# First keys in two transfers, four extra products ahead of the first transposes, and a later place for five value loads

## The chip, the cores and the metric

The kernel runs on one core of one Trainium2 chip. The metric is the device time of one execution in microseconds. TensorE (PE) multiplies, VectorE (DVE), ScalarE (ACT) and GpSimd (POOL) do the elementwise work, and transfers are issued by GpSimd's and SyncE's (SP) queues. The program is built under a manual schedule: each engine runs its instructions in the order in which the Python code issues them, and semaphores order the engines among each other.

## What is computed

Attention in a sliding window of 32 positions to either side, for 8 sequences of 576 positions with 8 heads of 64, then two matrix products with a gelu-like gate between them:

```python
def _attn_ref(q, k, v):
    scores = scale * np.matmul(q, k.transpose(0, 1, 3, 2))
    mask = np.abs(pos[:, None] - pos[None, :]) <= window      # window = 32
    scores = np.where(mask, scores, -1000000000.0)
    ...
    attn = attn / (np.sum(attn, axis=-1, keepdims=True) + 1e-09)
    return np.matmul(attn, v)

def _moe_ref(x, w_in, w_out):          # 4608 x 512, 512 x 2048, 2048 x 512
    h = x @ w_in
    g = h * (1.0 / (1.0 + np.exp(-1.702 * h)))
    return g @ w_out
```

## The kernel before

The 4608 rows (8 sequences of 576, one after the other) are cut into 36 units of 128 rows; four units make a tile of 512, nine tiles in all. For a unit, `scores` multiplies transposed keys by transposed queries, ScalarE exponentiates, `band` multiplies by a 0/1 mask, `values` multiplies by the values (with a column of ones that gives the sums), `norm` divides, `x_T` transposes the result. For a tile, layer 1 (512 to 2048) and layer 2 (2048 to 512) follow. From the second tile on both use a seven-product scheme for 2x2 blocks, whose sums VectorE forms; the first tile is multiplied plainly (`layer1_plain`, `layer2_plain`).

Queries and values are offset by 32 rows against each other. A unit's scores need keys of the unit and the first half of the next one. The values of a unit need `ve[u % 9]`, a ring of nine tiles, and `vo[u % 5]`, a ring of five that `odd_v` fills on GpSimd with the upper half of one value tile and the lower half of the next.

`opening` handles the first two tiles. `load_first` (L147) loads the keys and queries of the first tile in two parts each, several rows of a head on one partition; `setup_mask` (L99) makes the identity from an iota of GpSimd and a comparison of VectorE; `T_first` (L166) transposes on TensorE, four heads to a PSUM bank, and VectorE and ScalarE copy out. `seed` (L268) starts a score bank with a large negative bias by a product of the identity and the bias tile. `load_four` and `T_four` (L185, L193) do the same for the second tile. GpSimd issues all loads in one order: first keys, first queries, second part of both, values 0 to 4, then w_in in pieces, the second tile's keys and queries, the rest of w_in, more values, and w_out in four pieces.

Later units are loaded by `fetch(u)` (L722): queries of u, keys and values of u + 1. `T_pe` (L237) transposes units 8 to 12 on TensorE; `turn(u)` (L727) issues transposes by transfer on SyncE's queue for all later ones. `first_layer1` (L871) is layer 1 of the second tile; in its four rounds it copies odd values 8 to 11 and fetches 12 to 15. `run` (L809) then goes on with scores 8 to 15 and their values, and copies odd values 12 to 15 and fetches 16 there. `front` and `back` (L736, L764) repeat the pattern for the tiles from the third on. At most eight transfers of GpSimd are under way: each further one waits for the landing of the eighth before it. Each of the five buffers for queries and for keys comes free when its transpose has read it.

Of the kernel before, what the change touches and what calls it, by code (L numbers as in the profile page):

```python
# [15 lines left out]
F32 = mybir.dt.float32  # L16
BF16 = mybir.dt.bfloat16
# [9 lines left out]
class _Kernel:  # L27
# [55 lines left out]
    def setup(self):  # L83
        nc, cst = self.nc, self.cst
        self.ident = cst.tile([128, 128], BF16, name="ident")
        self.identh = cst.tile([128, 128], F16, name="identh")
        self.mask = cst.tile([128, 4, SQ], BF16, name="mask")
        self.bias = cst.tile([128, 512], BF16, name="bias")
        self.w1 = cst.tile([128, 4, self.DFF], F16, name="w1")
        self.w2 = cst.tile([128, 16, self.DM], F16, name="w2")  # L90
        self.a = {i: cst.tile([128, 2, 1024], F16, name=f"a{i}") for i in (1, 2, 3, 4)}
        self.b = {i: cst.tile([128, 8, 256], F16, name=f"b{i}") for i in (1, 2, 3, 4)}
        self.k_first = cst.tile([128, 4, 64], BF16, name="k_first")
        self.v_first = cst.tile([64, self.H, 66], BF16, name="v_first")
        self.ve = [cst.tile([128, self.H, 66], BF16, name=f"ve{i}") for i in range(9)]
        self.vo = [cst.tile([128, self.H, 66], BF16, name=f"vo{i}") for i in range(5)]
        self.spark = cst.tile([128, 1], F32, name="spark")

    def setup_mask(self):  # L99

        D = self.work.tile([128, 128], F32, name="gap", tag="s7", bufs=2)
        self.nc.gpsimd.iota(D, pattern=[[-1, 128]], base=0, channel_multiplier=1,
                            allow_small_or_imprecise_dtypes=True)
        dve = self.nc.vector
        dve.tensor_single_scalar(self.ident, D, 0.0, op=ALU.is_equal)
        dve.tensor_copy(self.identh, self.ident)
        for r in (slice(0, 64), slice(64, 128)):
            d = D[r, r].rearrange("p (b s) -> p b s", b=1).to_broadcast([64, 2, SQ])
            up = int(r.start > 0)
            for blk, op in ((2 * up, ALU.is_ge), (2 - 2 * up, ALU.is_le)):  # L110
                dve.tensor_single_scalar(self.mask[r, blk:blk + 2, :], d, 0.0, op=op)
# [35 lines left out]
    def load_first(self, c, part):  # L147
        if "first" not in self.stage:
            self.stage["first"] = self.sb("g", [128, self.H, 11, self.D], BF16, 2, "kq1")
        lo, n, j, at = self.FIRST[c][part]  # L150
        src = {"q": self.q, "k": self.k}[c]
        self.nc.gpsimd.dma_start(self.stage["first"][0:n // j, :, at:at + j],  # L152
                                 src[0, :, lo:lo + n, :].rearrange("h (p j) d -> p h j d", j=j))

    def kq_tile(self, t):

# [433 lines left out]

    SHARES = {("first", 1): (3, 0, 5, 4), ("first", 2): (3, 3, 6, 6), ("first", 3): (3, 1, 7, 7), ("last", 0): (0, 12, 6, 6),
              0: (4, 4, 6, 6), 1: (3, 3, 6, 6), 2: (0, 6, 5, 7), 3: (2, 1, 5, 4)}

    def opening(self):

        nc, dve, act, pool = self.nc, self.nc.vector, self.nc.scalar, self.nc.gpsimd
        self.setup()  # L600
        self.load_first("k", 0)
        self.load_first("q", 0)
        dve.memset(self.spark, 0.0)
        self.setup_mask()
        self.cut_mask()
        self.setup_bias()
        for t in self.ve:
            dve.memset(t[:, :, self.D:], 1.0)
        self.load_first("k", 1)
        self.load_first("q", 1)  # L610
        act.activation(self.spark, self.spark, AF.Exp)
        for u in (0, 1, 2, 3):
            self.load_v(u)
        self.load_v(4, slice(0, 1))
        self.load_w1(0, 256)
        self.load_w1(256, 256)
        self.load_w1(512)
        for u in (0, 1):
            self.odd_v(u, pool)
        self.load_w1(1024)  # L620
        for u in (2, 3):
            self.odd_v(u, pool)
        self.load_four("k")
        self.load_four("q")
        self.load_w1(1536)
        self.load_v(4, slice(1, 2))
        for u in (5, 6, 7, 8):
            self.load_v(u)
        for c in range(4):
            self.load_w2(c)  # L630
        self.T_first("k", 0, "AC", (dve, act))
        self.seed(0, "t")
        self.T_first("q", 0, ("LA", "LB"), (dve, act))
        self.seed(1, "AC")
        self.scores(0)
        self.scores(1)
        self.T_first("k", 1, ("LA", "LB"), (dve, dve))
        self.T_first("q", 1, ("B", "E"), (dve, act))
        self.seed(2, ("LA", "LB"))
        self.seed(3, "AC")  # L640
        self.scores(2)
        self.scores(3)
        self.values(0, "t")
        self.norm(0)
        self.values(1, ("B", "E"))
        self.norm(1)
        self.x_T(0, "LA", act)
        self.x_T(1, "LB", act)
        self.values(2, "t")
        self.norm(2)  # L650
        self.values(3, "AC")
        self.norm(3)
        h, n = ["LA", "LB", "A", "C", "B", "E"], [0]

        def l1(half, *fs, **kw):
            for f in fs:
                self.layer1_plain(0, f, half, h[n[0] % len(h)], **kw)
                n[0] += 1

        l1(0, 0)  # L660
        self.x_T(2, "B", act)
        self.x_T(3, "E", dve)
        l1(0, 2)
        l1(1, 0, 2)
        dve.tensor_copy(self.k_first, self.kT[0][:, :, 0:64])
        dve.tensor_copy(self.v_first, self.ve[0][0:64])
        l1(0, 4, 6)
        l1(1, 4, 6)
        for i in (3, 1, 2, 4):
            self.w1_sums((i,), 0)  # L670
        h[:], n[0] = ["LA", "LB", "C"], 0
        l1(0, 8)
        halo = self.kT[4]
        self.T_four("k", "BE", (dve, act))
        dve.tensor_copy(self.kT[4][:, :, 0:64], halo)
        l1(0, 10)
        act.activation(self.spark, self.spark, AF.Exp)  # L677
        self.T_four("q", "tA", (dve, act))
        gelus = []
        kept = [self.sb("s7", [128, 512], F32, 2) for _ in range(2)]  # L680
        room = self.sb("xs", [128, 2, 512], F32, 1, "room")
        kept += [room[:, i, :] for i in range(2)]
        l1(1, 8, later=gelus, kept=kept[0])
        l1(1, 10, later=gelus, kept=kept[1])
        for u in (4, 5, 6, 7):
            self.odd_v(u, pool)
        self.load_kq("k", 8)
        for u in (8, 9, 10, 11):
            self.fetch(u)
        h[:], n[0] = ["LB", "LA"], 0  # L690
        self.scores(4, "AC")
        self.scores(5, "t")
        l1(None, 12, later=gelus, kept=kept[2])
        self.scores(6, "BE")
        self.band(4)
        l1(None, 13, later=gelus, kept=kept[3])
        self.scores(7, "AC")
        self.values(4, "t")
        self.band(5)
        self.norm(4)  # L700
        h[:], n[0] = ["B", "E"], 0
        l1(None, 14, later=gelus)
        self.band(6)
        l1(None, 15, later=gelus)
        self.values(5, "t")
        self.norm(5)
        self.band(7)
        self.values(6, "AC")
        self.do(self.l2, 6)
        self.do(gelus)  # L710
        self.norm(6)
        self.values(7, "t")
        self.norm(7)
        self.do(self.l2, 2)
        for i in (3, 1, 2):
            self.w1_sums((i,), 1)
        self.x_T2(4, "A", act)
        self.do(self.l2, 8)
        self.x_T2(6, "t", dve)
        self.do(self.l2, 6)  # L720

    def fetch(self, u):  # L722
        self.load_kq("q", u)
        self.load_kq("k", u + 1)
        self.load_v(u + 1)

    def turn(self, u):  # L727
        self.T_dma("q", u)
# [35 lines left out]
    def back(self, t):  # L764
# [3 lines left out]
        u = 4 * t + 4  # L768
        bands = [lambda i=i: self.band(u + i) for i in range(4)] if more else []
        dv = bands[0:2]  # L770
        for n in range(4):
            self.turn(u + n + 4)
            self.fetch(u + n + 5)
            if t == 2 and n in (1, 3):
                self.values(u + n - 1, "t")
                self.norm(u + n - 1)
# [32 lines left out]
    def run(self):  # L809
        pool, act = self.nc.gpsimd, self.nc.scalar  # L810
# [20 lines left out]
        do(more, 4)  # L831
        self.values(8, "t")
        self.values(9, "AC")
        self.odd_v(12, pool)
        self.odd_v(13, pool)
        self.fetch(16)
        self.scores(11, "BE")
        self.norm(8)
        self.band(10)
# [16 lines left out]
        self.scores(15, "t")  # L856
        do(self.x_sums(2))
        self.seed2 = dve
        self.odd_v(14, pool)
        self.odd_v(15, pool)  # L860
        late = self.back(2)
        for t in range(3, self.NT):
            self.front(t, late)
# [7 lines left out]
    def first_layer1(self):  # L871

        dv = [lambda: self.w1_sums((4,), 1)]
        for n in range(4):
            if n == 3:
                self.turn(12)
                self.turn(13)
            self.odd_v(8 + n, self.nc.gpsimd)
            self.fetch(12 + n)

            def fill(i):
                self.do(self.l2, {1: 1, 7: 1, 2: 3, 4: 3}[i])
# [55 lines left out]
```

## Time and profile before

| | |
|---|---|
| three timed runs | 283.83, 285.00, 285.83 us |
| median | 285.0 us |
| profiled execution, its own time | 282.94 us |
| its span, first to last instruction | 281.2 us |
| instructions | 8890 |
| DVE busy | 212.2 us (75%) |
| ACT busy | 196.0 us (70%) |
| POOL busy | 132.1 us (47%) |
| software queue (GpSimd's), moved | 18.42 MB in 106656 packets |
| hardware queue (SyncE's and ScalarE's), moved | 18.10 MB in 43120 packets |
| output stores, 256 KB each, to landing | 4.8 us |

The page gives each engine's busy time, then the span in 40 slices with the busy share in tenths, the chain of work that ended last, and groups of instructions by source line with mean duration and the idle time before them. "L70" is the helper that issues every plain product, so those rows are told apart by the names of the tiles (output, then inputs). In the chain of waits each piece has its start, its length and the engine, tile and line that time ran over. In a timeline line the brackets hold the idle time before an instruction and what ended it. Transfers are listed with the time from issue to landing.

### The profile page before, as it was taken

The page shows a single profiled execution, that of the slowest core. Times are in us where ns is not written, and L with a number is a line of the kernel's source. Part 1 is how long each engine was busy: PE and PEld are TensorE (multiplying, and loading weights), DVE is VectorE, ACT ScalarE, POOL GpSimd, SP SyncE. Part 2 cuts the span into 40 slices and gives each one's busy share as a digit, 9 for nine tenths or more (in the row PEclk, how much of TensorE's full clock was granted, in tenths as well). Part 3 has the DMA queues.
Part 4 walks back from the last instruction along what each step waited for, and adds up shares of the span by engine and source line. Part 5 has one row for each costly group of instructions (what it writes and reads, how often), then busy time and mean ns, then how long its engine had stood idle before and what let it go on. Part 6 is the DMA issues. An engine that isn't in the chain of part 4 may idle for free.

```text
span 281.2 us, 8890 instructions
## 1 busy us (share of the span) xinstructions
PE 269.3 (96%) x3648; PEld 222.5 (79%) x3648; DVE 212.2 (75%) x491; ACT 196.0 (70%) x344; POOL 132.1 (47%) x199
## 2 busy tenths in 40 slices
PE   1979999999999999999999999999999999999994
PEld 1568656776888888888888888888888888888883
DVE  4464698897978888888888887888788888855631
ACT  2576893989897688658875887687759775667410
POOL 8894596998798570936094619442210000000000
PEclk9999999999999999999999999999999999999999
DMA  8999999999999999999999999999943051101033
GB/s 88 167 206 197 178 207 162 191 131 155 134 187 142 204 159 183 101 201 136 190 105 211 136 153 89 194 155 167 157 52 95 2 114 21 75 2 75 2 112 115
DMA packets 150265, 37.61 MB, mean 134 GB/s; under 512 B 138064, under 2 KB 145872, under 8 KB 150224
## 3 DMA queue, kind: packets, MB, share of 16 engines
q0 software_dynamic: 106656, 18.42, 95.3%
q1 hardware_dynamic: 43120, 18.10, 37.6%
q8 instruction: 28, 0.46, 0.7%
q10 hardware_dynamic: 448, 0.52, 0.6%
q14 instruction: 13, 0.11, 0.2%
HBM read 36.83 MB, written 9.44 MB: 165 GB/s over the span
## 4 chain that ended last, share of the span: by engine, by line
PE 91%; DVE 3%; ACT 3%; issue 1%; POOL 1%; POOLq 0%; DVEq 0%
PE o L70 40%; PE h L70 39%; PE sc L70 5%; PE pv L70 4%; DVE x L328 1%; ACT p L290 1%; PE tp L177 1%; PE tp L244 1%; ACT kq L67 1%; POOL kq L152 1%; PE tp L356 0%; ACT L677 0%; PE tp L344 0%; PE tp L201 0%; DVE rec L327 0%
## 5 line engine op out<-in xcount | busy, mean ns | idle before, releaser
L459 ACT ACTIVATE g<-h 128x512 f16<-128x512 f32 x128 | 72.2, 598 | 35.3 <-PE h L70 35.0
L70 PEld LDWEIGHTS <-g 128*128 128x128 f16 x576 | 54.5, 98 | 10.1
L222 POOL COPY vo<-ve 64x264 int32<-64x264 int32 x71 | 32.1, 452 | 63.5 <-PE pv L70 54.4
L70 PEld LDWEIGHTS <-a 128*128 128x128 f16 x512 | 49.5, 97 | 10.5 <-issue 0.3
L70 PE MATMUL h<-xs,a 128*128 128x256 f16 x384 | 57.6, 272 | 0.2
L70 PE MATMUL o<-w,g 128*128 128x256 f16 (+1 forms) x320 | 55.0, 294 | 0.0
L70 PE MATMUL h<-xT,w 128*128 128x256 f16 (+1 forms) x368 | 53.6, 277 | 0.0
L70 PEld LDWEIGHTS <-w 128*128 128x128 f16 x496 | 47.6, 98 | 7.4
L70 PEld LDWEIGHTS <-gs 128*128 128x128 f16 x384 | 36.9, 98 | 4.9 <-issue 0.2
L290 ACT ACTIVATE p<-sc 128x512 bf16<-128x512 f32 x72 | 37.0, 618 | 3.3 <-PE sc L70 3.1
L70 PE MATMUL o<-b,gs 128*128 128x256 f16 x256 | 37.6, 273 | 0.0
L70 PE MATMUL o<-b,g 128*128 128x256 f16 x256 | 37.5, 273 | 0.0
L211 POOL DMA_DIRECT2D ve<-in_v_dram x40 | 34.3, 868 | 6.3 <-DMA w<-in_moe_w_out_dram 2.1
L472 DVE TENSOR_TENSOR h<-h,s 128x512 f32<-128x512 f32 x32 | 22.3, 698 | 18.4 <-PE h L70 18.2
L67 ACT COPY h<-h 128x512 f32<-128x512 f32 x32 | 18.9, 590 | 17.3 <-PE h L70 16.9
L328 DVE TENSOR_TENSOR x<-pv,rec 128x256 f16<-128x256 f32 (+1 forms) x52 | 27.4, 527 | 1.8
L141 POOL DMA_DIRECT2D qst<-in_q_dram x35 | 28.0, 801 | 0.9 <-issue 0.5
L141 POOL DMA_DIRECT2D kst<-in_k_dram x31 | 26.5, 858 | 0.6 <-DMA w<-in_moe_w_out_dram 0.6
L478 DVE TENSOR_TENSOR h<-h,s 128x512 f32<-128x512 f32 x32 | 22.4, 699 | 4.8 <-PE h L70 4.2
L298 DVE TENSOR_TENSOR p<-p,mask 128x1024 bf16<-128x1024 bf16 x32 | 22.4, 700 | 0.1
L67 ACT COPY s<-h 128x512 f32<-128x512 f32 x32 | 19.2, 599 | 1.3
L70 PE MATMUL h<-xs,w 128*128 128x256 f16 x128 | 19.2, 273 | 0.0
(87 smaller groups left out, 339.4 us busy)
## 6 DMA issues: line engine op xcount, KB each, us to landing
out_dram<-o_sb SPq DMA_DIRECT2D x33, 256.0 KB, 4.8
ve<-in_v_dram POOLq DMA_DIRECT2D x32, 128.0 KB, 6.6
kst<-in_k_dram POOLq DMA_DIRECT2D x25, 128.0 KB, 6.4
qst<-in_q_dram POOLq DMA_DIRECT2D x21, 128.0 KB, 5.9
w<-in_moe_w_out_dram POOLq DMA_DIRECT2D x4, 512.0 KB, 11.1
w<-in_moe_w_in_dram POOLq DMA_DIRECT2D x3, 512.0 KB, 9.7
qst<-in_q_dram POOLq DMA_DIRECT2D x7, 96.0 KB, 5.5
kq<-in_q_dram POOLq DMA_DIRECT2D x2, 256.0 KB, 5.8
```

The source lines that it names most:

```text
L67: (eng.copy if eng is self.nc.scalar else eng.tensor_copy)(out, in_)
L70: self.nc.tensor.matmul(out, lhsT, rhs, start=start, stop=stop, skip_group_check=True)
L141: self.nc.gpsimd.dma_start(t[off:off + n], src[b, :, s:s + n, :].rearrange("h s d -> s h d"))
L152: self.nc.gpsimd.dma_start(self.stage["first"][0:n // j, :, at:at + j], src[0, :, lo:lo + n, :].rearrange("h (p j) d -> p h j d", j=j))
L211: self.nc.gpsimd.dma_start(t[off:off + n, :, :self.D], self.v[b, :, s:s + n, :].rearrange("h s d -> s h d"))
L222: eng.tensor_copy(*((words(vo[64:128]), words(self.ve[u % 9][64:128])), (words(vo[0:64]), words(nxt)))[i])
L290: self.nc.scalar.activation(p[:, eo].rearrange("k h s -> k (h s)"), sc[eo], AF.Exp, scale=self.scale)
L298: (eng or self.nc.vector).tensor_mul(pv, pv, msk.to_broadcast([128, 8, 2, SQ]))
L328: dve.tensor_mul(x[:, 4 * at:4 * (at + n), :].rearrange("p (b h) d -> p b h d", b=n), acc[:, :, :, :D], r.to_broadcast([128, n, 4, D]))
L459: act.activation(g[:, f, 256 * half:256 * half + 256], bank.rearrange("p (i n) -> p i n", i=2), AF.Gelu_apprx_sigmoid)
L472: dve.tensor_add(e, b, s7)
L478: dve.tensor_add(c, b, s7)
```

## The change

Four edits are made together. The first part of the first keys, until now one transfer of eight heads, goes in two transfers of four heads each. A new tile of 128 x 512 zeros is cleared by VectorE right after the identity is made, and four products of it with itself, into bank E, which nothing reads, stand ahead of the first transposes. `T_four("q")` stands behind one more half group of layer 1 (eight products). Value loads 13 to 17 leave the fetches of units 12 to 16 and are issued in one row behind the fetch of 16's queries and keys; the copies of odd values 8 to 11 stand behind the fetch of their round, those of 12 and 13 behind the row of value loads, and those of 14 and 15 behind the fetch of 17.

```diff
@@ setup, setup_mask
+        self.idle = cst.tile([128, 512], BF16, name="idle")
...
         dve.tensor_single_scalar(self.ident, D, 0.0, op=ALU.is_equal)
+        dve.memset(self.idle, 0.0)
         dve.tensor_copy(self.identh, self.ident)
@@ load_first
-        self.nc.gpsimd.dma_start(self.stage["first"][0:n // j, :, at:at + j],
-                                 src[0, :, lo:lo + n, :].rearrange("h (p j) d -> p h j d", j=j))
+        for h in (slice(0, 4), slice(4, 8)) if (c, part) == ("k", 0) else (slice(0, 8),):
+            self.nc.gpsimd.dma_start(self.stage["first"][0:n // j, h, at:at + j],
+                                     src[0, h, lo:lo + n, :].rearrange("h (p j) d -> p h j d", j=j))
@@ new
+    def keep_busy(self, n, tag):
+        junk = self.bank(tag, [128, 512], F32, "junk")
+        for _ in range(n):
+            self.mm(junk, self.idle[:, 0:128], self.idle, start=True, stop=True)
@@ opening
+        self.keep_busy(4, "E")
         self.T_first("k", 0, "AC", (dve, act))
...
-        self.T_four("q", "tA", (dve, act))
...
         l1(1, 8, later=gelus, kept=kept[0])
+        self.T_four("q", "tA", (dve, act))
         l1(1, 10, later=gelus, kept=kept[1])
@@ fetch
-    def fetch(self, u):
+    def fetch(self, u, v=True):
         self.load_kq("q", u)
         self.load_kq("k", u + 1)
-        self.load_v(u + 1)
+        if v:
+            self.load_v(u + 1)
@@ back
             self.turn(u + n + 4)
             self.fetch(u + n + 5)
+            if t == 2 and n == 0:
+                self.odd_v(14, self.nc.gpsimd)
+                self.odd_v(15, self.nc.gpsimd)
@@ run
         self.values(8, "t")
         self.values(9, "AC")
+        self.fetch(16, v=False)
+        for u in range(13, 18):
+            self.load_v(u)
         self.odd_v(12, pool)
         self.odd_v(13, pool)
-        self.fetch(16)
...
         self.seed2 = dve
-        self.odd_v(14, pool)
-        self.odd_v(15, pool)
         late = self.back(2)
@@ first_layer1
+            self.fetch(12 + n, v=False)
             self.odd_v(8 + n, self.nc.gpsimd)
-            self.fetch(12 + n)
```

## The prediction

> **What bounds the kernel now.** The page first: where is TensorE not working?
>
> ```profile
> span 281.2 us, 8890 instructions
> PE 269.3 (96%) x3648; PEld 222.5 (79%) x3648; DVE 212.2 (75%) x491; ACT 196.0 (70%) x344; POOL 132.1 (47%) x199
> ...
> PE   1979999999999999999999999999999999999994
> ...
> DMA  8999999999999999999999999999943051101033
> ```
>
> TensorE is idle before its first product and at the end; in between it is full. The transfers are full too until slice 30, so early loads land when the queue lets them, whatever TensorE does. The table by stretch, next, confirms it: 39.76 of 40 us busy from 20 to 60, 39.80 from 60 to 100. So what the kernel can gain lies in the first 20 us, and everything behind must keep up with an earlier start. The chain of waits in order of time shows those 20 us:
>
> ```profile
> 6.14 1.29 PE tp L177 x32
> 7.42 0.97 PE sc L70 x2
> 8.39 1.00 PE tp L177 x16
> 9.39 1.58 PE sc L70 x18
> 10.99 1.58 ACT p L290 x3
> 12.59 0.69 DVE kq L67
> 13.32 1.44 PE sc L70 x35
> ```
>
> From 6.14 to 10.97 the chain is TensorE alone, 4.84 us. How fast does it run there? The groups by shape from 6 to 12 us (first line) and from 13 to 15 us (second), which are the same seed products:
>
> ```profile
> L70 PE MATMUL sc<-bias,ident 128*128 128x512 bf16 x4 | 2.1, 621 | 0.0
> ...
> L70 PE MATMUL sc<-bias,ident 128*128 128x512 bf16 x4 | 1.2, 376 | 0.2 <-DVE kq L67 0.2
> ```
>
> 621 ns become 376; the transposes of 128 columns go from 311 to 219. The page's granted clock says 9 throughout, but the durations show a slow array until about 12.0 us, 5.9 us after its first product. Seeds, start to start, take 0.40 us each before and 0.215 after. So the opening is bound by a TensorE at half pace.
>
> What sets 6.13? The timeline:
>
> ```profile
> 1.29 0.87 POOL L152 DMA_DIRECT2D kq<-in_k_dram  x1 [0.84 <-POOLq L922]
> 3.14 0.26 POOL L102 IOTA gap<- 128x128 f32 x1
> 3.43 0.23 DVE L105 TENSOR_SCALAR ident<-gap 128x128 bf16<-128x128 f32 x1 [2.56 <-POOL gap L102]
> 3.69 0.55 DVE L106 CAST identh<-ident 128x128 f16<-128x128 bf16 x1
> 6.13 1.13 PEld L177 LDWEIGHTS <-kq 80*64 80x64 bf16 x32 [6.13 <-DMA kq<-in_k_dram]
> ```
>
> The identity is there at 3.66; the keys land at 1.29 + 4.8 (transfer table) = 6.09.
>
> **The change, part by part.** *Split of the first keys.* One issue of 0.87 becomes two. The nearest row is a 64-row issue, 0.69 (two in 1.39 at 53.77); two are 1.38, so +0.5 for everything behind on GpSimd's queue; ends 0 (each half costs half) and +0.87 (each costs the whole). Queued behind: first queries, iota, second keys, second queries, values. The first queries land at 2.16 + 5.3 = 7.5 and are first transposed at 8.32, so their 0.5 is hidden (without the 0.8 of cover it would be paid whole). Iota and identity come 0.5 later: 4.16. Later, GpSimd idles 0.50 at 12.46 for a landing, which swallows the rest. The first half of the keys can land up to 1 us sooner, but the new products hold TensorE until about 6.15, so I count that at nothing.
>
> *The zero tile.* A memset of 256 words per partition between identity and cast. Rows: 16-word memsets take 0.08 (four in 0.32 at 5.28); the 512-column bias takes 0.48. Ends 0.1 and 0.5, I take 0.3, nearer the bias by its width. It ends at 4.46. VectorE's setup is thus 0.8 later in all: the bias at 6.9 (needed 7.36), the last memsets at 7.1 against a first key copy at 6.94, 0.15 late, which has until the second seeds at 9.32: hidden.
>
> *Four products of 512 columns.* TensorE starts at 4.5 instead of 6.13, at slow pace: 4 x 0.41 = 1.64, done at 6.15, as the keys land. In-order cost on the transposes: 0.02, say 0.05. What they can bring is the pace. If the array speeds up a fixed 5.9 us after its first product, that is 10.4 instead of 12.0. Then the 48 score products from 10.29 take about 0.7 instead of 1.07 (the row at 14.06 has 0.70), so 0.3; the eight transposes before VectorE's copy at 11.98 take 0.21 instead of 0.43, another 0.2: the copy starts 0.55 earlier, the three copies run back to back (1.89), ScalarE's exponentials start 0.3 earlier, and the scores at 14.06 and all behind start 0.5 earlier. Lower end: no earlier pace, 0 to -0.05. Upper end: full pace from the first query transposes at 8.32 on. Then those save 0.45, the second seeds 0.4 (half under the copies), scores 0.4, transposes 0.2, less what the copies and exponentials keep: about 1.0. I take 0.55.
>
> The Trainium skill (TensorE: Matmul & The Clock Gate, Part 1) says that a monitor with a free-running window of about 3.4 us releases the clock after a busy window, and that the moment varies from run to run. By that, with an edge at 12.0, edges lie at 8.6 and 5.2; the window from 5.2 would now be full, and the pace would rise at 8.6.
>
> *Later transposes of the second queries (behind one more group of layer 1).* They ran at 29.27; the queries land at 17.83 + 11.0 = 28.8, 0.45 earlier. With an earlier start they would wait; now they come 0.97 later (8 products) and don't. What waits behind them: ScalarE's copy at 31.39, which already comes after its table load and spark (to 31.48), and then the scores at 32.43. The transposes' second half is now ready at about 31.4, the copy starts where it did: cost 0 (0 to +0.2).
>
> *Values 13 to 17 behind keys and queries.* Six issues, 1.40 + 0.88 + 0.89 + 0.90 + 0.91 = 4.98 us on GpSimd, move behind query 16 and key 17; copies of odd 12 and 13 behind them, 14 and 15 behind the fetch of 17. Who used the order: scores 15 run at 78.64 and need key 16, whose transpose is
>
> ```profile
> 73.09 1.19 SPq L235 DMA_TRANSPOSE kT<-kst  x1
> ```
>
> and in the transfer table of that moment (median us to landing last)
>
> ```profile
> kT<-kst SPq DMA_TRANSPOSE x1, 4.9
> ```
>
> so it lands at 78.0: 0.65 in hand. Three value loads (3.17) go from ahead of it; its buffer waits on key 13's transpose (65.9), which itself comes about 1 earlier, so I expect 1.5 to 3 more. On the other side the issue of value 17 waits for the products of values 8 (71.2 to 71.7), and the odd copies come behind it, near 76 instead of 69 to 72; values 12 are multiplied at 84.27, values 14 at 95.03: 8 us of cover. Cost now: 0; the part only keeps a gain from being lost.
>
> **How much gets through.** Loads land at fixed times: w_out's third quarter at 31.49 + 11.2 = 42.7 against its product at 43.48 (index 16 of the second layer), the first at 37.5 against 38.64. So 0.8 is let through, and a 1.0 would be cut to 0.8 unless the whole stream starts earlier. Sum: -0.55 + 0.05, about -0.5 in the forecast, 280.7 span; +0.2 to -1.0 at the ends. The profiled run's own time was 282.94, span 281.2; the three timed runs are 283.83 to 285.83, median 285.0, 2.1 higher. I take the difference over unchanged, 284.4, and a shade more for the waits below: 284.3.
>
> **Rivals.**
> *Full pace from the first query transposes on.* The upper end above, cut to 0.8 by w_out or let through to 1.0: 284.0 to 284.2. For: in before the array sped up after its first long unbroken stretch of work, 8.32 to 12.0, and now one begins at 4.5. Against: only one rise is seen, so no row says how long a stretch is needed. This is where the clock page's windows would put it.
> *No earlier pace.* The zero products end, and the pace still rises near 12: 285.0. For: in before, 2.2 us of work from 6.13 to 8.32 were not enough. Against: work is continuous from 4.5.
> *The timed runs already wait for key 16.* They are 0.9 to 2.9 above the profiled one, and the cover at scores 15 is only 0.65; loads that land 1 to 2 later would stall TensorE there. Then the reordering gives 1 to 2 more: 282.3 to 283.5. Against: nothing in the profile waits there.
> *Slower: the zero tile comes late.* The cast at 3.69 took 0.55 and ended at 4.24, when GpSimd's issue ended (4.21). If the memset is held in the same way until the end of the second keys' issue (about 4.85) or the next (5.75), the four products end at 6.55 or 7.4: +0.4 to +1.2 on the transposes, 285.4 to 286.2 if the pace gains nothing. It decides from a memset end after 4.46. Against: the small memsets at 5.28 ran while GpSimd issued.
>
> **Chances.** Forecast 0.43, full pace from the queries 0.2, no earlier pace 0.13, timed waits removed 0.15, slower 0.09. Range: from the waits' 282.5 to just above the late tile's lower value, 285.5; some 2 in 10 lie outside. One per cent is 2.85 us, about what can be told from no change: faster needs under 282.15, only the waits' far end (0.06); slower needs over 287.85, twice the late tile's worst (0.03).
>
> **What would show it.** Right: four products of about 0.6 us from 4.5, first transposes at 6.1 to 6.3, seeds at the fast 376 before 10.4, scores' second pair 0.5 earlier, layer 1 running from about 19.8 instead of 20.34, key 16's transpose landing by 76.5, and an unchanged tail. Wrong: a memset ending past 4.6, slow seeds at 9.3 followed by slow transposes at 11.3, a new TensorE wait for w_out near 42 to 43, or GpSimd's odd copies released after 84.

## The result, and the profile after

The changed kernel takes 285.97 us (median of 20 runs, 284.41 to 287.1) against 283.76 for the kernel before (20 runs, 282.74 to 286.65): ratio 1.0061, 95% interval 1.0041 to 1.0082. By the ratio that is about 1.7 us slower (the medians differ by 2.2): inside the one per cent that the prediction held to be hard to tell from no change, though the interval leaves 1 out, and above the range of the forecast, which was for a small gain. The profiled execution took 286.94 us, the second highest of its twenty, and that of the kernel before 282.94, below its median. So the two profiles lie further apart than the times, and the waits read from them are on the long side: the span is 285.1, 3.9 more than before.

The page of the changed kernel, span, engines, TensorE and transfers by slice:

```profile
span 285.1 us, 8900 instructions
...
PE 271.2 (95%) x3652; PEld 222.5 (78%) x3652; DVE 212.3 (74%) x492; ACT 196.2 (69%) x344; POOL 134.3 (47%) x200
...
PE   3979999999999987999999999999999999999995
...
DMA  7999999999999999999999999999934140201023
```

TensorE's busy time rose by 1.9 us, about what the four products take (1.89), but the span by 3.9. Two digits in the middle, 8 and 7, are new: slices of 7.1 us each from 100 to 114 us. That is far behind every edit. The timeline of TensorE there, and of VectorE's one long wait:

```profile
106.21 0.24 PE L70 MATMUL sc<-qT,kT 64*64 64x64 bf16 x2 [0.87 <-DMA qT<-qst]
106.86 0.44 PE L70 MATMUL sc<-qT,kT 64*64 64x64 bf16 x22 [0.41 <-DMA kT<-kst]
...
111.11 0.61 PE L70 MATMUL h<-xs,a 128*128 128x256 f16 x4 [1.52 <-DVE xs L391]
```

```profile
110.63 0.42 DVE L391 TENSOR_TENSOR xs<-xT 128x512 f16<-128x512 f16 x1 [4.08 <-DMA xT<-x]
```

TensorE waits for transposed queries and keys (scores 19), and then for VectorE, which waits 4.08 us for transposed results. All three are transposes by transfer on SyncE's queue. Start to start, beyond the length of the products, these places cost 1.04, 0.59, 1.69 and (at 111.89) 0.24 us, together 3.6. In the kernel before nothing there costs over 0.16. Layer 1 starts at 18.65 instead of 18.22. Matched product by product, the changed kernel runs 0.15 us late from 20 us on, 0.6 late from a wait for w_out's first quarter at 38.9, 0.9 late from 77 to 104 (scores at 101.98 instead of 101.08), and 4.3 late behind the waits above (a product of layer 1 at 112.24 instead of 107.92). So most of the longer span arises in these eight microseconds, and some 0.8 between 20 and 77 us.

Why were the transposes late? Queries and keys of a unit are loaded by GpSimd before SyncE can transpose them. GpSimd's timeline, before and then after:

```profile
77.55 1.36 POOL L141 DMA_DIRECT2D qst<-in_q_dram  x2
...
81.73 0.88 POOL L141 DMA_DIRECT2D qst<-in_q_dram  x1
```

```profile
79.66 0.40 POOL L225 COPY vo<-ve 64x264 int32<-64x264 int32 x1 [2.07 <-DMA ve<-in_v_dram]
80.21 1.36 POOL L143 DMA_DIRECT2D qst<-in_q_dram  x2
...
83.37 3.44 POOL L225 COPY vo<-ve 64x264 int32<-64x264 int32 x6
86.76 0.88 POOL L143 DMA_DIRECT2D qst<-in_q_dram  x1
```

Queries 17 are issued at 80.21 instead of 77.55, behind a copy of odd 13 that waits for values 14; queries 18 at 86.76 instead of 81.73, behind six copies for odd 14 to 16. The busy share of the transfers between 85 and 100 us, in 40 slices of 0.375 us, before and then after, shows the hole that stands ahead of the issue of queries 18, at 85.8 to 87.2:

```profile
DMA  9999999999999619999999999999999999999999
```

```profile
DMA  9931008926899999999995999999999999999999
```

SyncE issues in order. Queries 17 land at 85.98 instead of 83.75, so their transpose, and everything behind it, goes out later; the second transpose of results lands at 110.54 instead of 105.66. That was the first theory (A); its first half, that the place of the odd copies is the cause, did not stand.

The opening of the changed kernel, TensorE:

```profile
4.57 1.89 PE L70 MATMUL junk<-idle 128*128 128x512 bf16 x4 [4.57 <-DVE idle L107]
6.39 1.29 PE L180 MATMUL tp<-ident,kq 80*64 80x80 bf16 x32
...
9.58 0.68 PE L70 MATMUL sc<-bias,ident 128*128 128x512 bf16 x2
...
12.21 0.64 PE L180 MATMUL tp<-ident,kq 128*64 128x128 bf16 x16 [0.68 <-DMA kq<-in_q_dram]
```

The pace is full at 9.58 (two seeds in 0.68 instead of 1.03), but at 12.21 TensorE waits for the second part of the queries, which landed at 12.16 (before 10.41). Second keys came at 10.67 (8.95), values 0 at 13.09 (11.36), w_out's third quarter at 44.17 (42.66).

### The profile page after: what moved, and what is told of

It is laid out like the page before. It is cut to its first block, busy times and chain, and to the rows that moved or that the text cites. A ratio compares the mean times of both kernels' runs of the same rounds, so it can differ in the third digit from the quotient of the medians.

```text
span 285.1 us, 8900 instructions
## 1 busy us (share of the span) xinstructions
PE 271.2 (95%) x3652; PEld 222.5 (78%) x3652; DVE 212.3 (74%) x492; ACT 196.2 (69%) x344; POOL 134.3 (47%) x200
## 4 chain that ended last, share of the span: by engine, by line
PE 80%; DMA 13%; POOL 4%; DVE 1%; issue 1%; ACT 1%; POOLq 0%; DVEq 0%
PE o L70 38%; PE h L70 34%; DMA w<-in_moe_w_out_dram 4%; PE pv L70 4%; DMA xT<-x 3%; DMA o_sb<-in_k_dram 3%; PE sc L70 3%; DMA ve<-in_v_dram 2%; POOL ve L214 2%; POOL kq L155 1%; PE tp L247 1%; POOL vo L225 1%; PE tp L359 0%; DVE xs L391 0%; ACT p L293 0%
## 5 line engine op out<-in xcount | busy, mean ns | idle before, releaser
L225 POOL COPY vo<-ve 64x264 int32<-64x264 int32 x71 | 33.6, 473 | 63.5 <-PE pv L70 49.9
L70 PEld LDWEIGHTS <-g 128*128 128x128 f16 x576 | 54.6, 98 | 10.4
```

The source lines that it names most:

```text
L70: self.nc.tensor.matmul(out, lhsT, rhs, start=start, stop=stop, skip_group_check=True)
L225: eng.tensor_copy(*((words(vo[64:128]), words(self.ve[u % 9][64:128])), (words(vo[0:64]), words(nxt)))[i])
```

## The experiments

All ratios are to the kernel before, measured beside each run, with 95% intervals. Three theories stood at the start. A: the moved values and odd copies make the queries and keys of 18 to 20 late, which is the loss at 105 to 112. B: the opening's late loads carry on to there. C: the split slows the stream of loads.

**One part at a time.** *e1*: only the values and odd copies moved.

```diff
+            self.fetch(12 + n, v=False)
             self.odd_v(8 + n, self.nc.gpsimd)
-            self.fetch(12 + n)
...
+        self.fetch(16, v=False)
+        for u in range(13, 18):
+            self.load_v(u)
         self.odd_v(12, pool)
         self.odd_v(13, pool)
-        self.fetch(16)
```

> Kernel before with only the value loads and odd copies moved. Theory A (the reordering makes the loss: TensorE stands about 3.3 us near 105 to 112 because queries 18 to 20 and keys 19, 20 are issued 3 to 5 us later behind six odd copies): about 2 to 3.3 us slower than before (ratio 1.007 to 1.012), a wait of TensorE for the transposes of queries and keys at scores 18 and 19 and for the sums of the fourth tile's x. Theory B (the opening's later transfers cause those waits): within 0.3 us of before, no such waits.

The diff shows only part of it: the hunks of the change in `fetch` and `back` and the lines that leave `run` belong to it too. Measured 285.23 us, ratio 1.0044 [1.0017, 1.0072]; the loads of the opening land as before, and the waits stand at 105.3 to 110: 0.20, 0.19, 0.75 and 0.24 us. Theory A's place is right, its size here 1.4 us, below the 2 to 3.3 that were expected.

*e2*: only the opening (split, products, later transposes of the second queries; the diff of the change without its hunks in `fetch`, `back`, `run` and `first_layer1`).

> Kernel before with the split, the products and the later transposes of the second queries, values in their old order. Theory A: no waits near 105; the opening is even or up to 0.5 us better, ratio 0.998 to 1.001. Theory B: the loss stays, ratio 1.006 to 1.01.

284.49 us, 1.001 [0.9983, 1.0036]: no loss that can be measured, and no wait at 105. Theory B falls for that place. But the profile has another wait, at scores 15:

```profile
80.86 0.44 PE L70 MATMUL sc<-qT,kT 64*64 64x64 bf16 x22 [1.70 <-DMA kT<-kst]
```

Key 16 was late, as it was in *e3* below (0.49 us). From 20 to 72 us the products of e2 had run 0.12 us ahead of those before the change. The changed kernel has no such wait. So the moved values did serve key 16, and lost more behind it.

*e3*: only the split.

```diff
-        self.nc.gpsimd.dma_start(self.stage["first"][0:n // j, :, at:at + j],
...
+        for h in (slice(0, 4), slice(4, 8)) if (c, part) == ("k", 0) else (slice(0, 8),):
+            self.nc.gpsimd.dma_start(self.stage["first"][0:n // j, h, at:at + j],
```

> Kernel before with only the first keys in two transfers. Theory C (the split costs the transfer stream: the software queue moved some 120 KB less between 4 and 9 us): second keys land near 10.5 instead of 8.95 and w_out's third quarter near 44 instead of 42.7; 0 to 1 us slower, ratio 1.000 to 1.004. Theory D (the split is free and the products or the later setup slow the stream): second keys within 0.5 us of 8.95, ratio 1.000.

284.53 us, 1.0006 [0.9981, 1.0031]. Second keys land at 10.26, first queries at 8.81, w_out's third quarter at 42.97. Theory C is right for the second keys (10.5 expected), too large for w_out (44 expected, 42.66 before), and the delay is too small to show in the time.

*e4*: only the zero tile and the four products (`setup`, `setup_mask`, `keep_busy` and its call in `opening`, of the change).

> Kernel before with only the zero tile and the four products. Theory C: transfers land as in before (second keys near 8.95), the array speeds up about 2 us sooner, layer 1 starts its unbroken run 0.4 to 0.8 us sooner, ratio 0.997 to 0.999. Theory D: second keys later by a microsecond or more, no gain.

284.22 us, 0.9994 [0.9968, 1.002]. The pace rises at 9.54, but falls back. The windows of this run, columns start:end, length, busy time by engine with instructions in brackets, TensorE clock, transfer share, GB/s:

```profile
12.95:16.36 3.41, 1.78 (x84) 1.40 (x84) 1.93 (x6) 2.06 (x4) 3.08 (x8) 1.00 1.64 189
16.37:19.78 3.41, 3.05 (x44) 2.41 (x44) 1.63 (x6) 2.36 (x3) 3.41 (x5) 0.50 1.25 207
```

After 3.41 us with TensorE busy 1.78, the next 3.41 us run at 0.50, and layer 1 starts at 18.38, no sooner than before (18.22); its unbroken run, expected 0.4 to 0.8 sooner, comes 0.2 later.

**Where the odd copies stand.** *e5*: the changed kernel with odd 14 and 15 behind the fetches of 18 and 19; *e6*: also odd 13 behind the fetch of 17 (the diff is that of e6; e5 has `n in (1, 2)`).

```diff
-            if t == 2 and n == 0:
-                self.odd_v(14, self.nc.gpsimd)
-                self.odd_v(15, self.nc.gpsimd)
+            if t == 2 and n < 3:
+                self.odd_v(13 + n, self.nc.gpsimd)
...
         self.odd_v(12, pool)
-        self.odd_v(13, pool)
```

> The changed kernel, whole, but GpSimd's copies of odd values 14 and 15 stand behind the fetches of 18 and 19 and no longer both ahead of the fetch of 18. Theory A (the queries and keys of 18 to 20 come late because they stand behind odd copies): queries 18 issued about 84.5 us instead of 86.76 (before: 81.73), since four copies leave that place but queries 17 still wait until about 80 for the odd copy 13; TensorE's waits at 105 to 112, 3.3 us in the changed kernel, shrink by the 2.2 us that the issue comes earlier, to about 1; time about 284 us, ratio to before 0.999 to 1.001. Theory B (the late loads of the opening carry on to there): the waits at 105 to 112 stay over 2.5 us and the ratio near 1.006.

> As the run before, and the copy of odd 13, which waits in the changed kernel until 79.66 us for the landing of values 14, stands behind the fetch of 17. Theory A: queries 17 issued at about 77 us instead of 80.21 and queries 18 near 82, as early as before the change (77.55 and 81.73); no TensorE wait over 0.3 us from 100 to 115; what is left is the opening's own effect, so time 282.5 to 283.5 us, ratio 0.994 to 1.0. Theory B: the waits stay, ratio 1.004 or more.

286.33 us, 1.0069 [1.0037, 1.0101], and 286.54, 1.0056 [1.0026, 1.0086]. Nothing is won back. In e5 queries 18 go out at 85.27, and 1.32 us of wait stand at 78.5 and 1.22 at 109.3. In e6 queries 17 were issued at 77.00, 3.2 us sooner than in the change, and landed at 87.02 and 87.23 (two pieces), 1.2 later: they stood in the queue behind six value transfers, the last of which landed at 86.16. An early issue is not an early landing. Theory A's form, that the copies' place is the cause, falls.

**Keeping the pace.** *e7* is e4 with two further groups of products; *e8* the whole change without the split, with these groups and the odd copies of e6.

```diff
         self.norm(1)
+        self.keep_busy(4, "LA")
         self.x_T(0, "LA", act)
+        self.keep_busy(4, "LB")
         self.x_T(1, "LB", act)
```

> The kernel before with the four products ahead of the first transposes, and two further groups of four such products in the gaps around the transposes of the first two results (14.4 to 16.7 us, where TensorE was busy 1.73 of 3.3 us). Theory D (the array falls back to half pace after a stretch of 3.4 us with too much idle time, as the record from 16.37 to 19.78 showed with the four products alone): no record of half pace after about 10 us, layer 1 starts 0.3 to 0.6 us sooner than the 18.4 of the four products alone, unbroken work from about 19.8 us; ratio 0.997 to 0.999, if no key or weight is then waited for. Rival: the fall back hangs on something else than idle time (a fixed number of stretches after the start): the half pace comes again at 16 to 17 us, ratio 1.0 or above by the eight extra products.

> The whole change without the split of the first keys, with the copies of odd 13, 14 and 15 behind the fetches of 17, 18 and 19, and with the two further groups of products. Theory (A and D together, and C, that the split makes the loads land up to 1.7 us later): w_out's third quarter lands at 42.7 us or before instead of 44.17, no TensorE wait over 0.3 us at 78, 105 or 110, half pace not after 10 us, span 280.2 to 281, ratio 0.994 to 0.998, the lowest of the four. If the split costs nothing it is equal to the run with the three copies moved, within 0.002. If a wait for w_out takes its place, it shows at 38 to 44 us and the ratio is 0.999 or above.

e7: 284.85 us, 1.0011 [0.9988, 1.0033]. No fall back, but the first rise came only at 11.55, and the groups held the transposes up: layer 1 starts at 20.04. In the trace they cost more than they could give, and the time shows neither gain nor loss, so this says little about e7's theory D, that idle stretches make the pace fall. e8: 285.94, 1.0042 [1.0015, 1.0068]; the same start at 20.04, the first loads within 0.35 us of those before the change, no wait at 105, but 1.46 us at scores 15. So its loss stands in another place than that of the others.

**What in the row of values costs.** Theory F: GpSimd reaches key 16 before its buffer is free and waits 2.6 us in the change (3.6 in e1), with the values behind it. Theory G: the odd copies that wait for landings. *e9* is e1 with seven key buffers; *e12* is its control; *e10* is e1 with all odd copies from 13 on three rounds later; *e11* is e1 with values 13 to 15 back in their fetches. The edits, in the order e9 and e12, e10, e11:

```diff
-        t = self.stage[c, u] = self.sb(c + "st", [128, self.H, self.D], BF16, 5)
+        t = self.stage[c, u] = self.sb(c + "st", [128, self.H, self.D], BF16, 7 if c == "k" else 5)
```

```diff
-            if u + n + 4 < self.NU:
-                self.odd_v(u + n + 4, self.nc.gpsimd)
+            if u + n + 1 < self.NU:
+                self.odd_v(u + n + 1, self.nc.gpsimd)
```

```diff
-            self.fetch(12 + n, v=False)
+            self.fetch(12 + n, v=n < 3)
...
-        for u in range(13, 18):
+        for u in (16, 17):
             self.load_v(u)
```

> The kernel before with the moved values and odd copies alone (ratio 1.0044), and seven buffers for keys instead of five. Theory F (the reordering makes GpSimd reach key 16 before the transpose by transfer has freed its buffer, 3.6 us of waiting at 61.97 in the run with the values alone, and the values stand behind it, so the stream loses 0.2 to 0.3 MB by 70 us that it does not win back): no wait of GpSimd over 1 us between 60 and 70 us, values 17 landed at about 81 instead of 83.56 (before 80.63), no TensorE wait over 0.3 us at 105 to 110, ratio 0.998 to 1.001. Theory G (odd copies that wait for landings hold queries 18 and later behind them): the wait at key 16 goes, but queries 18 are still issued 2 us later than before (81.73) and the ratio stays 1.003 or above.

> The moved values alone, five key buffers, and from unit 13 on every odd copy three rounds later than in the kernel before (odd 13 behind the fetch of 17, odd 16 behind that of 20), so that none waits for a landing. Theory G: GpSimd idles less than 0.5 us between 76 and 92, queries 18 issued by 81, ratio 0.998 to 1.001. Theory F: the wait of 2.5 to 3.6 us at key 16 stays, values 17 land at 83 or later, queries 17 and 18 land late although they are issued early (as queries 17 did with odd 13 moved: issued 77.00, landed 87.02), ratio 1.003 to 1.006.

> The moved values alone, but values 13 to 15 back in the fetches of 12 to 14; only values 16 and 17 stand behind queries 16 and keys 17, the odd copies as in the change. Theory F: three value issues (2.7 us) fill the time in which GpSimd waited for key 16's buffer, so that wait falls under 1 us, values 17 land by 81.5, ratio 0.998 to 1.002. Theory G: odd 14 to 16 still stand ahead of queries 18, which are issued 2 us or more after 81.73; ratio 1.003 or above.

> The kernel before with seven key buffers instead of five and nothing else. No key waits for its buffer there between 60 and 70 us, so both theories expect no change: ratio 0.998 to 1.002, no new TensorE wait over 0.4 us. If it is faster by 0.003 or more, the run with seven buffers and the moved values says nothing by itself, and is to be compared with this one.

e9: 285.61 us, 1.0044 [1.0006, 1.0081]. Key 16 no longer waits, yet values 17 land at 83.37 and the waits are 1.20 us at 78.4 and 1.10 at 106:

```profile
63.33 0.89 POOL L141 DMA_DIRECT2D kst<-in_k_dram  x1
```

e12: 285.01, 1.0033 [1.0006, 1.006], where no change was expected. No TensorE wait in the trace explains it, but the profiled execution (283.40) was the fastest of its twelve. So what the buffers do by themselves stays open, and since e9 is not told from e12, its time says nothing about F. Its trace says that the waits at 78 and 106 come without the wait at key 16 too: that wait is not the only cause of them.

e10: 289.18, 1.0183 [1.0138, 1.0228]. Queries 18 go out at 79.22, sooner than before the change; but queries 17 landed at 86.1, behind the values again, and TensorE waited 1.69 us for transposed queries and 1.32 for keys at 104 to 108. G as the only cause falls. It is also the slowest of all; in the profiled execution the array lost its pace for 6.8 us behind these waits:

```profile
103.36:106.77 3.41, 1.37 (x31) 0.78 (x29) 1.88 (x5) 2.59 (x6) 0.97 (x2) 1.00 1.80 136
106.78:113.60 6.82, 5.85 (x47) 4.25 (x48) 2.36 (x6) 1.66 (x3) 6.62 (x10) 0.50 1.84 194
```

e11: 283.95, 0.9994 [0.996, 1.0028]. Values 17 land at 79.3, queries 17 at 82.9, no wait at 105 to 112, although odd 14 to 16 stand ahead of queries 18 as in the change. Three loads back in their places undo the loss. They shorten both things at once: GpSimd idles 0.62 us at most at a time from 60 to 85 us, and no odd copy ahead of queries 18 waits for a landing.

**The link.** Theory H: queries 17 behind the row hold SyncE's transposes. Rival I: odd copies that need the late values hold queries 18. *e13* is e1 with queries 17 and keys 18 ahead of values 16 and 17, *e14* the same in the whole change, *e15* without the split; *e17* is e13 with the late odd copies of e10 as well.

```diff
         for u in range(13, 18):
+            if u == 16:
+                self.fetch(17, v=False)
             self.load_v(u)
...
-            self.fetch(u + n + 5)
+            if (t, n) == (2, 0):
+                self.load_v(18)
+            else:
+                self.fetch(u + n + 5)
```

> The moved values alone (ratio 1.0044, queries 17 issued 77.26, landed 84.5, their transpose issued 84.69, last result transpose landed 108.50), but queries 17 and keys 18 issued ahead of values 16 and 17. Theory H: queries 17 land at 80 to 82 us, their transpose is issued by 83.9 as in the kernel before, the second result transpose lands by 106.5 (before 105.66), no TensorE wait over 0.4 us at 105 to 110, ratio 0.998 to 1.001. Rival I (the values themselves come too late, whoever stands ahead of them: odd copies that need them hold queries 18): queries 17 land early but queries 18 are issued after 83.5 and land after 88, the waits at 105 to 110 stay at 0.7 us or more, ratio 1.003 or above.

> The whole change with queries 17 and keys 18 ahead of values 16 and 17. Theory H: the 3.3 us of waits at 105 to 112 fall under 1 us, ratio 0.996 to 1.001. Rival I, or if the opening's late loads are what carries on: waits over 2 us stay there and the ratio is 1.004 or above.

> The same without the split of the first keys. Theories H and C: loads of the opening as in the kernel before, no wait for key 16 and none at 105 to 112, ratio 0.995 to 0.999, the best of all runs if the four products' gain of up to 0.5 us is then let through. Rival: the earlier start is met by the next late load; ratio 0.999 to 1.003.

> The moved values alone, with both cures: queries 17 and keys 18 ahead of values 16 and 17, and every odd copy from 13 on three rounds later. Theory K (two links, each enough by itself: queries 17 behind the row of values, and odd copies that wait for values 16 and 17 ahead of queries 18): queries 17 land at about 82 and queries 18, issued by 81, before 88 us; the second result transpose lands by 106.5; TensorE waits at 103 to 110 under 0.5 us; ratio 0.998 to 1.002. Rival J (loads that run ahead of what is needed slow the transposes by transfer, which took 8 to 9 us in the run with the late odd copies against 5 to 7 before): queries land early, yet the result transposes land after 108 and the waits stay over 1.5 us, ratio 1.006 or above.

e13: 285.33 us, 1.0049 [1.0023, 1.0076]. Queries 17 land at 82.2 and their transpose goes out at 82.37, sooner than before the change (83.89). Then the other link closes:

```profile
85.77 1.32 POOL L222 COPY vo<-ve 64x264 int32<-64x264 int32 x3 [3.88 <-DMA ve<-in_v_dram]
87.13 0.88 POOL L141 DMA_DIRECT2D qst<-in_q_dram  x1
```

The copies wait 3.88 us for values 16 (landed at 85.65), queries 18 follow at 87.13 (before 81.73), and the waits stand at 104.7 to 110.6: 0.97, 0.32, 1.18, 0.24. That is rival I. e14: 285.48, 1.0053 [1.0025, 1.0082], with TensorE idle 0.98, 0.37 and 1.22 us at 105 to 111; e15: 285.89, 1.0076 [1.0048, 1.0105], with 1.83 us at 78.6 and 1.44 at 109.9.

e17: 286.84, 1.0092 [1.0056, 1.0128]. Both links are out of the way at the issue: queries 17 land at 81.8, sooner than before the change (83.7), and queries 18, issued at 79.50, at 88.0 (before 86.6). Yet values 19, issued at 81.83, land at 94.6, keys 20 at 98.7 and the second result transpose at 108.81:

```profile
106.30 0.44 PE L70 MATMUL sc<-qT,kT 64*64 64x64 bf16 x22 [1.72 <-DMA kT<-kst]
```

That is rival J by its numbers. Its mechanism, that loads running ahead slow the transposes, is not shown; theory K falls as a full account. One combination was not run. GpSimd still waits 2.05 us at key 16's buffer in e17 (2.72 in e10), and e9, without that wait, keeps the odd copies that wait for landings. So F and G together, each enough by itself, remain a rival that no run excludes.

**Split another way.** *e16*: two transfers of 40 partitions and eight heads.

```diff
+        cut = (slice(0, 40), slice(40, 80)) if (c, part) == ("k", 0) else (slice(0, n // j),)
+        for r in cut:
+            self.nc.gpsimd.dma_start(self.stage["first"][r, :, at:at + j],
+                                     src[0, :, lo + j * r.start:lo + j * r.stop, :].rearrange("h (p j) d -> p h j d", j=j))
```

> The kernel before with the first keys in two transfers of 40 partitions with all eight heads each, in place of four heads each on 80 partitions. If four heads a transfer is what slowed the stream, second keys land at 8.9 to 9.5 us (one more issue of at most 0.7) instead of 10.26, and w_out's third quarter near 42.7. If it is the second transfer, second keys land after 10 us as with the split by heads, and the bytes moved from 5 to 7 us fall by a third again. Time within 1 % of the kernel before by either.

One time, 284.65 us; second keys at 10.13, w_out's third quarter at 43.71. Scores 15 wait 1.71 us for key 16. So the late landing comes with the second transfer, whichever way the load is divided; part of it is the later issue of the second keys (4.13 in e16, 3.89 in e3, 3.32 before). The bytes of the packets that the software queue started from 5.0 to 7.5 us, summed, are 454 KB before, 349 in e3, 399 in e16: a dip of 12 % by rows, 23 % by heads. One profile each; neither expectation fits whole.

**The undo in the whole change.** *e18*: the changed kernel, values 13 to 15 back in their fetches (the edit of e11).

> The whole changed kernel (ratio 1.0061), but values 13 to 15 back in the fetches of 12 to 14. If the row of values is the cause in the whole change as it was alone (1.0044 to 0.9994): no TensorE wait over 0.5 us at 105 to 112, ratio 0.998 to 1.002; key 16 may be waited for at scores 15 again by up to 0.6 us, as in that run. If the opening's late loads carry on: waits over 1 us at 105 to 112 or 1.9 us at scores 15, ratio 1.003 or above.

283.89 us, 0.9994 [0.9973, 1.0015]. The interval lies clear below that of the change. Scores 19 run through, and 0.24 us is the longest wait near scores 15:

```profile
105.88 0.70 PE L70 MATMUL sc<-qT,kT 64*64 64x64 bf16 x48
```

What the transfers did in the stretch ahead of the waits, the windows of the kernel before, of the changed one and of e18:

```profile
88.00:106.00 18.00, 17.96 (x267) 15.16 (x267) 15.47 (x35) 13.30 (x26) 13.04 (x20) 1.00 1.91 170
```

```profile
88.00:106.00 18.00, 17.23 (x240) 14.33 (x238) 15.57 (x35) 12.98 (x24) 14.15 (x22) 1.00 1.99 149
```

```profile
88.00:106.00 18.00, 17.89 (x246) 14.91 (x242) 15.26 (x34) 12.45 (x23) 14.09 (x21) 1.00 2.26 169
```

The last number is GB/s: 170, 149, 169. The ten kernels with values 13 to 15 in the row, e8 left out, have 140 to 158 in that window, all others (e8 too) 167 to 175. In the change more than half of the difference lies at 100 to 105 us (121 GB/s against 162 before; at 88 to 100 it is 171 against 175), where TensorE was only 0.9 us behind. So the lower rate comes ahead of TensorE's waits, but behind the late issue of queries 18: a mark of the loss, not shown to be its cause. No kernel of these beats the one before by more than its interval; e18, e11 and e4 (0.9994 each) are equal to it.

## Why the prediction was wrong

The forecast of 284.3 started from 284.4 for the kernel unchanged; the twenty runs of that kernel give 283.76. That base explains none of the miss: it made the forecast too high, and the result is higher still.

*Values 13 to 17 behind keys and queries* is the step that failed. It was put at cost 0, "8 us of cover", by asking who multiplies values 12 and 14. Nobody had to wait for those, and none did. It did not ask what stands behind the row on GpSimd's queue: the copies of odd 12 and 13, queries 17, the copies of odd 14 to 16, which need the row's last values, then queries 18 to 20, whose transposes SyncE issues in order with those of the results. Shown: the row with values 13 to 15 in it makes the loss (e1, 1.0044), and without them it is gone, alone (e11) and in the whole change (e18). Shown as links, each present in a trace: queries 17 landing behind the row (e6, e10), and odd copies waiting for the row and holding queries 18 (e13). Open: why taking away both links (e17) or the wait at key 16's buffer (e9, whose control e12 was slow as well) did not bring the time back; the two together were not tried. The common mark of nearly all is the lower rate of transfers from 88 to 106 us; what keeps it low was not isolated.

The text named odd copies "released after 84" as a sign of being wrong. They ran from 83.37 to 86.8; the sign was right, and it had no price in the sum. In the chances the failing case was missing: the slower rival was the zero tile, not the queue.

*What was right in that step.* The row leaves key 16 in time: scores 15 wait 1.89 us with the new opening and values in their old places (e2), and not in the change. The cover of 0.65 was rightly seen as thin (in e3, e16 and e2 the split alone or the new opening used it up). But "1.5 to 3 more" was too much: key 16's transpose landed at 77.76, not by 76.5.

*Four products.* Right in the start (4.57 against 4.5) and in bringing the pace, 9.76 against the forecast 10.4. A little short in size: 1.82 us from their start to that of the transposes, where 1.64 was counted, so the transposes came at 6.39, 0.26 later than before instead of 0.05. The term's mechanism, a fixed 5.9 us after the first product, failed: over the 20 profiles of this study the rise comes 3.7 to 8.7 us after it. The gain of 0.55 did not arrive at layer 1, at 18.65 with the change and 18.38 with the products alone, against 18.22. In the change the second queries landed too late; with the products alone the pace fell back. With the whole opening alone (e2) the products from 20 us on came 0.12 sooner.

*Split of the first keys.* Put at nothing, hidden. Its extra issue was hidden, but the loads behind it landed up to 1.75 us later in the change (second queries; 0.4 for the first of w_in, 1.5 for w_out), so "loads land at fixed times" did not hold. Mis-sized: by itself (e3) the split moved the second keys by 1.3 and w_out's third quarter by 0.3 us, and its time is not told from that before; what else delayed w_out in the change was not isolated.

*Zero tile* and *later transposes.* Right: the memset took 0.27 us against 0.3 and ended at 4.51 against 4.46, beside GpSimd's issues, so the slower rival falls. The wait at 32 us is 0.36 before and after.

*How much gets through.* The w_out cover of 0.8 was right in kind: with the later loads TensorE stood 0.33 us at 38.9, ahead of the product with w_out's first quarter, landed at 39.22; from 34 to 40 us the kernel fell from 0.15 to 0.61 us behind.

*The other rivals.* "Full pace from the query transposes on" and "no earlier pace" are both within what the scattered moment of the rise allows; an early rise moved little (8.96 in e2, 0.12 us gained). "The timed runs already wait for key 16" is not borne out: with the values moved and the old opening nothing became faster (e1, e11).

## What to carry to other kernels

A load that is moved back in an in-order queue is paid by everything that is issued behind it, and by every copy on the issuing engine that waits for its landing: follow the next two or three loads to their users, not only the user of the moved one. Cover counted at one user (key 16) and not at the next (queries 17 and 18) turned a wait of up to 1.9 us at one place into 3.6 us at another. To judge such a move, look at the landing times rather than the issue times, and at the transfers' rate in the stretch behind it as a mark.

## What was not expected of the hardware

*The pace falls back in the middle of work.* The clock records of this case, but for the last of a run, last 3.41 us or multiples of it. Six of the 20 profiles fell to half pace for one such stretch that began at 16.4 to 18.8 us. In the stretch before it TensorE had been busy 1.46 (e15), 1.48 (e18), 1.78 (e4), 2.11 (e12), 2.12 (e1) or 2.24 us (e6) of 3.41. Others as little filled did not fall: 1.98 (e5, from 13.86) and 1.88 (the changed kernel, from 108.75). So the busy time of the stretch alone does not decide. After waits near 104 to 108 us, e10 ran 6.83 and e17 3.41 us at half pace. The Trainium skill (TensorE: Matmul & The Clock Gate, Part 1) gives the same window, 3413 ns and free-running; it lets the pace fall after at least one idle window, where here windows over half busy were enough. With a window that runs freely the first rise would come at scattered moments, as it does: in 16 of the 20 profiles 3.65 to 6.35 us after the first product, in four 7.6 to 8.7.

*A queue that lands late what is issued early.* In e6 the first piece of queries 17 was under way for 10.0 us (issued 77.00, landed 87.02), against 5.5 for the same piece before the change (77.55, 83.03).
